# Regrouping the small products of a DeltaNet and maxout kernel between its large ones, with two chunks in one PSUM tile

## The chip, the cores and the metric

The kernel runs on one core of a Trainium2 chip. The time is device microseconds (us) of one execution. The engines are PE (TensorE matrix products; PEld is its weight load), DVE (VectorE), ACT (ScalarE), POOL (GpSimd) and SP (SyncE, which here only issues transfers). Each engine works through its own instructions strictly in order and waits on semaphores for the others. Lower is better.

## The reference

Two stages follow each other. First a delta rule attention, token by token, for 4 batches (B), 8 heads (H), 768 tokens (S) and head size 48 (D):

```python
k_n = k / (norm(k) + 1e-6)
for t in range(S):
    y[:, :, t] = einsum('bhd,bhde->bhe', q[:, :, t], state)
    v_old = einsum('bhde,bhd->bhe', state, k_n[:, :, t])
    state += beta[t] * einsum('bhd,bhe->bhde', k_n[:, :, t], v[:, :, t] - v_old)
```

Then y, seen as 3072 tokens of 384 numbers, goes through a maxout layer of width 768 and an output product:

```python
h = maximum(maximum(x @ w1, x @ w2), x @ w3)
out = h @ w_out
```

All numbers are float32.

## The kernel before

**Attention in chunks.** The 768 tokens are cut into 12 chunks of 64. Inside a chunk, the recurrence becomes the inverse of a triangular matrix per head, so that a chunk needs only small products. A *unit* is one chunk and one half of the batches; 4 units (2 chunks) form a *group*, and there are 6 groups. The names of the steps, which are also the letters in the schedule below, are:

- `t` (`turn_blocks`, L375): transposes of keys and queries on DVE, from the tile `turned` that `load_blocks` (L348, letters `L` and `N`) fetched, into `kqt`.
- `g` (`gram`, L395): products of keys with keys and with queries, PSUM tile `p_g`; DVE makes `pt` from it (L390), ACT `at` (L423), and SP writes `at` to device memory as `at_d` (four transfers a unit, L436).
- `blocks(m)` (L478): one transfer from SP reads `at_d` back as `x_bl` in another layout (L483).
- `solve(m)` (L498): the triangular inverses of the 32-wide blocks. It begins with a norm (ACT's `root_bl`, L261, then a row of short DVE instructions) and goes on in 31 steps of two DVE instructions (L552, L556). Then SP writes `y_d` (L577) and reads it back as `ut` (L586, four transfers a chunk).
- `z` (`join_z`, L694): for each chunk 32 products of 32 x 32 into PSUM tile `p_z` (64 records in the trace, since each product shows as two), then two ACT copies into `z`.
- `d` (`turn_t1`, L615): transposes of `ut` on DVE.
- `j` (`join_u`, L707): 32 products from `z` and `d`'s result into `p_j`, then two ACT multiplications by -1 into `ut`.
- `k`, `q` (`old_k` L738, `old_q` L747): products of keys and queries with the running state, `p_k` and `p_q`; DVE subtracts the one from `v_t` (L743), ACT copies the other (L751).
- `u` (`new`, L753), `s` (`step`, L771), `y` (`to_y`, L793): new values, state update, outputs. `x`, `w`, `X`: y goes through device memory into the layout of the maxout stage, `xt`.

**The maxout stage.** `ffn(m)` (L1150) is a generator over the 512 tokens of group m. Each of its *steps* (a yield) computes one product of 128 x 512 outputs, `p_h`, three products deep (L1161), and its elementwise part: ACT's relu (L1171) on even steps, DVE's maximum (L1175) on odd ones. From group 1 on there are 12 such steps, 0 to 11, and then steps 12 to 19 for the output product `p_o` (L1199). Its PSUM tiles have two buffers, so the product of step 11 needs the maximum of step 9 to be done.

**The order is written by hand.** The outer loop (L1427) runs over m and, behind each step i of `ffn(m)`, calls `links(m + 1, LINKS[i])`: a string of letters with numbers. Letters of the recurrence act on group m + 1, loads and key products on the group after that. While the maxout of one group runs, the recurrence of the next one and the preparation of the one after next are so threaded between its products. Each string that holds products is one *place* of small products between large ones. Besides, the loop issues `blocks(m + 2)` behind step 6, starts `solve(m + 2)` behind step 8, takes three of its steps behind each later step and the last three behind step 0 of the next group.

Groups 1 to 4 run as four similar periods. Group 0 has its own schedule (`EARLY_LINKS`), in which `z` of chunks 2 and 3 stands behind step 18. The last group has no recurrence left.

**PSUM.** The small products share one rotation of three tiles: `ps_two(name)` (L83) gives a tile of 128 x 2 x 512 numbers. A chunk's z or j uses a quarter of a tile on each side: columns 0 to 255 of each of the two parts. A new tile waits until the one three before it has been read.

Of the kernel before, what the change touches and what calls it, by code (L numbers as in the profile page):

```python
# [18 lines left out]
BL = 32  # L19
# [4 lines left out]
def kernel(  # L24
# [31 lines left out]
    nc = tc.nc  # L56

    B, H, S, D = q.shape
# [24 lines left out]
    def ps_two(name):  # L83
        return psum.tile([128, 2, 512], FP32, name=name, tag="two", bufs=3)
# [103 lines left out]
    t1 = [const.tile([128, 2, H, BL], FP32, name=f"t1{i}") for i in range(NU)]  # L188
# [206 lines left out]
    def gram(n, parts=(0, 1), queues=one_queue, copy=nc.scalar.copy, later=False):  # L395
        kqt, g = kqts[n], n % 2
        p_g = ps_two("p_g")

        whole = len(parts) == 2 and not g
        for j in range(NP):  # L400
            for par in range(2):
                for bb in range(2):
                    kq = kqt[dims(par), j, bb ^ g]
                    for i in (0,) if whole else parts:
                        c0 = j * 128 + i * C
                        nc.tensor.matmul(  # L406
                            p_g[
                                rows(bb ^ (g * i)), par, c0 : c0 + C * (1 + whole)
                            ],
                            kq[:, 0],  # L410
                            kq if whole else kq[:, i],
                        )
        p_v = p_g.rearrange("p two (j i t) -> p two j i t", j=NP, i=2)
        if 1 in parts:
            pt = pts[n] = square("pt")
            if later:
                copy(by_par(pt), p_v[:, :, :, 1])
            else:
                masked(pt, p_v[:, :, :, 1])
        if 0 not in parts:  # L420
            return
        at = ats[n] = square("at")
        copy(by_par(at), p_v[:, :, :, 0])  # L423
        if queues:
            to_dram(n, queues)
# [52 lines left out]
    def blocks(m, queue=nc.sync):  # L478
        if m == 1:
            xs[m] = in_wo(0)  # L480
        else:
            xs[m] = work.tile([128, 2, HB * BL + HB], FP32, name="x_bl", bufs=1)
        queue.dma_start(  # L483
            out=in_rows(xs[m]),
            in_=at_d[m].rearrange("c f b h j i -> (c f b h) j i"),
        )
# [125 lines left out]
    def block(bb, f=0, n=BL):  # L612
        return slice(C * bb + BL * f, C * bb + BL * f + n)
# [23 lines left out]
    def heads_of(c, name, w):  # L637


        copies = (nc.scalar.copy,) if c else (nc.scalar.copy, nc.vector.tensor_copy)  # L640
        n = H // len(copies)
        for i, copy in enumerate(copies):
            p_v = ps_two(name)[:, :, 0 : n * w]
            yield (
                range(i * n, i * n + n),
                p_v.rearrange("p g (h x) -> p g h x", x=w), copy,
            )

    def negated_of(c, name, w):
        if c:  # L650
            p_v = ps_two(name)[:, :, 0 : H * w].rearrange("p g (h x) -> p g h x", x=w)
            yield range(H), (p_v, p_v), (nc.scalar.mul,) * 2
            return
        p = [
            ps_two(name)[:, :, 0 : NP * w].rearrange("p g (h x) -> p g h x", x=w)
            for _ in range(3)
        ]
        yield range(NP), (p[0], p[0]), (nc.scalar.mul,) * 2
        yield range(NP, H), (p[1], p[2]), (nc.scalar.mul, nc.vector.tensor_scalar_mul)

    def span(hs):
        return slice(hs[0], hs[-1] + 1)
# [15 lines left out]
    def halves_u(c):  # L678
        t, z = fine.pop(c), zs[c % NU]
        for hs, p_v, negate in negated_of(c, "p_f", BL):  # L680
# [4 lines left out]
            for f in (0, 1):  # L685
                for bb in range(2):
# [4 lines left out]
                        -1.0,  # L691
                    )

    def join_z(c):  # L694
        at = [ats.pop(2 * c + g) for g in range(2)]
        z, second = zs[c % NU], ut[c % NU][:, :, :, BL:C]
        for hs, p_v, _ in heads_of(c, "p_z", BL):
            for i, h in enumerate(hs):
                for bb, g in TILES:
                    r = block(bb, 1)  # L700
                    nc.tensor.matmul(
                        p_v[block(bb ^ g), g, i], at[g][r, h, 0:BL], second[r, g, h]
                    )
            for bb in range(2):
                nc.scalar.copy(z[block(bb), :, span(hs)], p_v[block(bb)])

    def join_u(c):  # L707
        z, t = zs[c % NU], t1[c % NU]
        u12 = ut[c % NU][:, :, :, BL:C]
        for hs, p_v, negate in negated_of(c, "p_j", BL):  # L710
            for i, h in enumerate(hs):
                for bb, g in TILES:
                    r = block(bb ^ g)
                    nc.tensor.matmul(p_v[bb][block(bb), g, i], t[r, g, h], z[r, g, h])  # L714
            for bb in range(2):
                negate[bb](u12[block(bb), :, span(hs)], p_v[bb][block(bb)], -1.0)
# [174 lines left out]
    def both_layers(t):  # L891
        p_m = ps_ffn([128, DM], "p_m")
        for f in range(FT):
            nc.tensor.matmul(  # L894
                p_m,
                w_sb[0][:, t, f * 128 : (f + 1) * 128],
                wo_sb[:, f],
                start=(f == 0),
                stop=(f == FT - 1),
            )  # L900
        nc.scalar.copy(w_sb[0][:, t, 0:DM], p_m)
# [146 lines left out]
    def cross_hidden(i):  # L1048


        n = PAIRS * 128
        w = w_sb[i]
        b11, b12 = w[:, 0, 0:n], w[:, 0, n : 2 * n]
        b21, b22 = w[:, 1, 0:n], w[:, 1, n : 2 * n]
        t = [
            work.tile([128, 2, n], FP32, name="crossed", tag="w_bits", bufs=5)
            for _ in range(2)
        ]
        t1, t2, t3, t4 = (t[n // 2][:, n % 2] for n in range(4))
        for to, a, b in ((t3, b22, b12), (t1, b12, b11), (t2, b22, t1), (t4, b21, t2)):  # L1060
            nc.vector.tensor_tensor(out=to, in0=a, in1=b, op=ALU.subtract)
        thirds[i] = dict(
            b11=b11, b21=b21, b22=b22, t1=t1, t2=t2, t3=t3, t4=t4,
            c1=w[:, 2, 0:n], c2=w[:, 2, n : 2 * n],
        )
# [147 lines left out]
    def some(gen, n):  # L1213
        for _ in range(n):
            if next(gen, gen) is gen:
                break
# [74 lines left out]
    for _ in range(2):  # L1291
        fetch(nc.gpsimd)
    halves_u(0)
    turn_t1(0)
    join_z(0)
    masked(pts[0], by_par(pts[0]))
    placed(1, 2)
    join_u(0)
    masked(pts[1], by_par(pts[1]))
    old_k(0)  # L1300
# [14 lines left out]


    LINKS = {
        0: "k0 q0 t0 L3", 1: "t1", 2: "g0 g1 t2", 3: "z0 z1 d0 d1", 4: "j0 j1 t3 V0",
        5: "g2 g3 p1", 6: "u0 N0", 7: "V1 N1", 8: "s0 y0 N2", 9: "x0", 10: "k1 q1",
        11: "u1 w0", 13: "y1 x1 s1", 14: "X0 w1", 16: "P0", 17: "X1 K0 K1 K2 K3",  # L1320
    }
    LAST_LINKS = {**LINKS, 17: "", 19: "X1"}
# [13 lines left out]

    RECURS = dict(
        z=join_z, j=join_u, k=old_k, q=old_q, u=new, s=step, y=to_y, x=to_x,
        e=halves_z, f=halves_u, d=turn_t1,
    )  # L1340
# [3 lines left out]
        g=lambda n: gram(n, queues=(nc.gpsimd,) * 2 if n in (10, 11) else one_queue),  # L1344
# [3 lines left out]
    def links(m, names):  # L1348
        for name in names.split():
            f, i = name[0], int(name[1])  # L1350
            if f in RECURS and m < GROUPS:
                RECURS[f](2 * m + i)
            elif f in MADE and m + 1 < GROUPS:
                MADE[f](2 * (m + 1) + i)
            elif f in UNIT and m + 1 < GROUPS:
                UNIT[f](4 * (m + 1) + i)
            elif f == "N" and m + 2 < GROUPS:
                load_blocks(4 * (m + 2) + i)
# [68 lines left out]
    for m in range(1, GROUPS):  # L1427
        for i, _ in enumerate(ffn(m)):
            if i == 0:
                some(solving, 3)  # L1430
            if m == 1 and i in (2, 5, 8):
                both_layers(i // 3)
            if m == GROUPS - 2 and i in (4, 5):
                cross_hidden(i - 3)
            if m == GROUPS - 2 and i in (8, 9):
                cross_weights(i - 8)
            if m + 2 < GROUPS:
                if i == 6:
                    blocks(m + 2)
                if i == 8:  # L1440
                    solving = solve(m + 2)
            links(m + 1, (LAST_LINKS if m == GROUPS - 2 else LINKS).get(i, ""))
            if i > 7:
                some(solving, 3 if i > 8 else 1)
# [29 lines left out]
```

## Time and profile before

| | |
|---|---|
| three runs | 513.08, 513.89, 513.96 us; median 513.89 us |
| profiled execution | span 510.5 us from first to last instruction; its own time around it is not given |
| mean granted TensorE clock | 0.966 |
| PE busy | 491.1 us, 96% of the span |
| DVE, ACT, POOL busy | 349.9, 168.7, 192.7 us |
| maxout products `p_h` (L1161) | 187.5 us, x450 |
| output products `p_o` (L1199) | 65.3 and 25.2 us |

How it is read: times are from the start of the span. The chain is followed back from the last instruction, at each step to what released it; its pieces add up to the span. In the timeline, a line gives start, duration, engine, source line, operation, output and inputs, count, and in brackets how long the engine had stood idle before and what ended that. "SPq" is the issue of a transfer by SP, not the transfer. Matrix products are pipelined, and their ends are modelled.

The windows of the four periods: 158.0 to 242.4 us (84.4 us long; it has three further products of the weights, `p_m`, in it), 242.4 to 315.0 (72.6), 315.0 to 387.7 (72.7), and group 4 from 387.7 on, which has no key products.

### The profile page before, as it was taken

The page shows a single profiled execution, that of the slowest core. Times are in us where ns is not written, and L with a number is a line of the kernel's source. Part 1 is how long each engine was busy: PE and PEld are TensorE (multiplying, and loading weights), DVE is VectorE, ACT ScalarE, POOL GpSimd, SP SyncE. Part 2 cuts the span into 40 slices and gives each one's busy share as a digit, 9 for nine tenths or more (in the row PEclk, how much of TensorE's full clock was granted, in tenths as well). Part 3 has the DMA queues.
Part 4 walks back from the last instruction along what each step waited for, and adds up shares of the span by engine and source line. Part 5 has one row for each costly group of instructions (what it writes and reads, how often), then busy time and mean ns, then how long its engine had stood idle before and what let it go on. Part 6 is the DMA issues. An engine that isn't in the chain of part 4 may idle for free.

```text
span 510.5 us, 18528 instructions
## 1 busy us (share of the span) xinstructions
PE 491.1 (96%) x8016; PEld 333.1 (65%) x8016; DVE 349.9 (69%) x801; ACT 168.7 (33%) x320; POOL 192.7 (38%) x317
## 2 busy tenths in 40 slices
PE   7778989999999999999999999999999999999996
PEld 6567778756565565665555565555655556998796
DVE  5897799969996430899563987635897455456752
ACT  5585664884422242210252101252101412113210
POOL 7434372783491926670575770503130000000000
PEclk9755999999999999999999999999999999999999
DMA  8938869764055925353675454923343202230001
GB/s 111 192 64 221 194 151 155 195 199 100 5 148 140 175 46 130 99 143 83 144 136 130 120 137 94 174 37 92 80 116 81 44 3 64 54 71 2 0 17 46
DMA packets 106304, 53.49 MB, mean 105 GB/s; under 512 B 89712, under 2 KB 99984, under 8 KB 106224
## 3 DMA queue, kind: packets, MB, share of 16 engines
q1 hardware_dynamic: 94352, 31.35, 30.4%
q0 software_dynamic: 9472, 20.37, 16.4%
q8 instruction: 63, 1.03, 0.9%
q10 hardware_dynamic: 2400, 0.59, 0.6%
q14 instruction: 17, 0.14, 0.1%
HBM read 39.17 MB, written 13.11 MB: 102 GB/s over the span
## 4 chain that ended last, share of the span: by engine, by line
PE 73%; DVE 14%; DMA 5%; ACT 4%; SPq 2%; issue 2%; POOL 0%; DVEq 0%; ACTq 0%; POOLq 0%
PE p_h L1161 26%; PE p_o L1199 13%; PE p_o L960 9%; PE p_e L1102 3%; DVE tmp L552 3%; PE p_g L406 3%; PE p_c L1102 2%; PE p_m L894 2%; PE p_u L759 2%; DMA kmore<-in_k_dram 2%; PE p_k L731 2%; PE p_y L801 2%; DVE y_bl L556 2%; PE p_s L782 2%; PE p_j L714 1%
## 5 line engine op out<-in xcount | busy, mean ns | idle before, releaser
L1161 PE MATMUL p_h<-xt,w_sb 128*128 128x512 f32 (+1 forms) x450 | 187.5, 558 | 0.7 <-ACT xt L827 0.6
L1161 PEld LDWEIGHTS p_h<-xt,w_sb 128*128 128x128 f32 x450 | 82.3, 193 | 68.7 <-issue 61.8
L1199 PE MATMUL p_o<-wo_sb,h 128*128 128x384 f32 x192 | 65.3, 490 | 0.0
L1175 DVE TENSOR_TENSOR h<-h,p_h 128x512 f32<-128x512 f32 (+1 forms) x42 | 25.4, 606 | 53.9 <-PE p_h L1161 52.8
L552 DVE TENSOR_TENSOR tmp<-x_bl,y_bl 128x31 f32<-128x31 f32 (+20 forms) x139 | 51.3, 369 | 4.1
L556 DVE TENSOR_TENSOR y_bl<-y_bl,tmp 128x31 f32<-128x31 f32 (+20 forms) x139 | 48.5, 349 | 4.8
L1199 PEld LDWEIGHTS p_o<-wo_sb,h 128*128 128x128 f32 x192 | 35.7, 190 | 23.2
L364 POOL DMA_DIRECT2D turned<-in_q_dram x72 | 39.1, 551 | 4.3 <-POOL turned L359 2.9
L1205 ACT COPY o_sb<-p_o 128x384 f32<-128x384 f32 x16 | 7.7, 479 | 85.8 <-PE p_o L1199 79.8
L1171 ACT ACTIVATE h<-p_h 128x512 f32<-128x512 f32 x24 | 14.3, 597 | 63.4 <-PE p_h L1161 60.5
L254 POOL TENSOR_TENSOR w_sb<-mant,up 128x384 int32<-128x384 int32 x18 | 19.1, 1059 | 39.3 <-DVE mant L250 39.2
L406 PEld LDWEIGHTS p_g<-kqt 48*64 48x64 f32 x1216 | 24.6, 142 | 9.0 <-issue 6.4
L406 PE MATMUL p_g<-kqt 48*64 48x64 f32 (+1 forms) x1216 | 27.8, 242 | 0.9 <-ACT kqt L335 0.8
L789 DVE TENSOR_TENSOR st<-st,p_s 48x768 f32<-48x768 f32 (+1 forms) x18 | 17.1, 949 | 15.4 <-PE p_s L782 15.2
L120 POOL DMA_DIRECT2D kpad<-in_k_dram x32 | 21.8, 690 | 14.1 <-issue 12.7
L1199 PE MATMUL p_o<-w_sb,xt 128*128 128x384 f32 x72 | 25.2, 486 | 0.0
L139 POOL DMA_DIRECT2D v_t<-in_v_dram x14 | 11.5, 829 | 35.5 <-PE p_u L759 35.5
L390 DVE TENSOR_TENSOR pt<-p_g,mask 128x512 f32<-128x512 f32 x20 | 13.8, 688 | 15.9 <-PE p_g L406 15.8
L287 POOL TENSOR_TENSOR v_t<-v_t,nrm 128x768 f32<-128x768 f32 x12 | 17.9, 1493 | 9.0 <-DVE nrm L281 8.9
L359 POOL MEMSET turned<- 128x96 f32 x18 | 3.3, 192 | 47.6 <-DVE kqt L380 47.6
L759 PEld LDWEIGHTS p_u<-v_t,ut 64*64 64x64 f32 x768 | 13.4, 141 | 10.1 <-issue 7.8
L1199 PEld LDWEIGHTS p_o<-w_sb,xt 128*128 128x128 f32 x72 | 13.7, 190 | 9.5
(212 smaller groups left out, 837.0 us busy)
## 6 DMA issues: line engine op xcount, KB each, us to landing
out_dram<-o_sb SPq DMA_DIRECT2D x40, 96.0 KB
w_bits<-in_moe_w_dram SPq DMA_DIRECT2D x9, 384.0 KB
w_bits<-in_moe_w_dram POOLq DMA_DIRECT2D x9, 384.0 KB, 5.2
turned<-in_q_dram POOLq DMA_DIRECT2D x72, 48.0 KB, 2.9
kpad<-in_k_dram POOLq DMA_DIRECT2D x32, 96.0 KB, 6.1
y_x<-y SPq DMA_DIRECT2D x16, 192.0 KB
qall<-y_x SPq DMA_DIRECT2D x32, 96.0 KB
v_t<-in_v_dram POOLq DMA_DIRECT2D x14, 192.0 KB, 5.0
```

What stands on the lines that cost most here:

```text
L120: queues[bb].dma_start(out=dst[rows(bb ^ g), :, 0:D], in_=src[2 * bb + g, :, c * C : (c + 1) * C, :].rearrange("h p d -> p h d"),)
L254: nc.gpsimd.tensor_tensor(out=dst.bitcast(I32), in0=mant_v.bitcast(I32), in1=up_v, op=ALU.add)
L364: (queue, nc.gpsimd)[i].dma_start(out=t[p0 : p0 + 32, bb, at : at + NP * 2 * D].rearrange("p (j x) -> p j x", j=NP), in_=(k, q)[i][2 * bb ...
L406: nc.tensor.matmul(p_g[rows(bb ^ (g * i)), par, c0 : c0 + C * (1 + whole)], kq[:, 0], kq if whole else kq[:, i],)
L552: nc.vector.tensor_tensor(out=t_v, in0=row.to_broadcast(t_v.shape), in1=column.to_broadcast(t_v.shape), op=ALU.mult,)
L556: nc.vector.tensor_tensor(out=rest, in0=rest, in1=t_v, op=ALU.subtract)
L759: nc.tensor.matmul(p_v[rows(bb ^ g), g, i], ut[c % NU][rows(bb), g, h], rhs[rows(bb), g, h],)
L960: nc.tensor.matmul(to[:, g], a[j][:, 128 * g : 128 * (g + 1)], b[j], start=(start and g == j == 0), stop=(stop and g == 1 and j == PAIRS - 1),
L1102: nc.tensor.matmul(to, w[stays], moves, start=(n == 0), stop=(n == len(terms) - 1))
L1161: nc.tensor.matmul(p_h, w_sb[i][:, t, f * 128 : (f + 1) * 128], xt[:, t, lo : lo + w], start=(t == 0), stop=(t == KT - 1),)
L1175: nc.vector.tensor_tensor(out=h, in0=h, in1=p_h, op=ALU.max)
L1199: nc.tensor.matmul(p_o, stays, moves, start=(n == 0), stop=(n == len(terms) - 1))
```

## The change

Three edits go together. First, `z` of the two chunks of a group takes one PSUM tile instead of two: the even chunk takes columns 0 to 255 of both parts, the odd one 256 to 511 (from chunk 2 on). The same is done for `j` (from chunk 4 on). Second, the strings of `LINKS` are regrouped: `k0 q0` move from step 0 to step 3, behind `z0 z1 d0 d1`; `g0 g1 t2` from step 2 to step 4, behind `j0 j1`; `t3` from step 4 to step 5; `g2 g3` from step 5 to step 6, behind `u0`. Third, `blocks(m + 2)` moves from step 6 to step 7. The number of places with small products falls from ten (steps 0, 2, 3, 4, 5, 6, 8, 10, 11, 13) to seven (3, 4, 6, 8, 10, 11, 13). The products and elementwise instructions themselves are the same.

```diff
+    shared = {}
+
+    def half_of(c, name):
+        key = name, c // 2
+        p = shared.pop(key) if key in shared else shared.setdefault(key, ps_two(name))
+        at = H * BL * (c % 2)
+        return p[:, :, at : at + H * BL].rearrange("p g (h x) -> p g h x", x=BL)
+
     def join_z(c):
         at = [ats.pop(2 * c + g) for g in range(2)]
         z, second = zs[c % NU], ut[c % NU][:, :, :, BL:C]
-        for hs, p_v, _ in heads_of(c, "p_z", BL):
+        if c < 2:
+            parts = heads_of(c, "p_z", BL)
+        else:
+            parts = [(range(H), half_of(c, "p_z"), None)]
+        for hs, p_v, _ in parts:
...
     def join_u(c):
         z, t = zs[c % NU], t1[c % NU]
         u12 = ut[c % NU][:, :, :, BL:C]
-        for hs, p_v, negate in negated_of(c, "p_j", BL):
+        if c < 4:
+            parts = negated_of(c, "p_j", BL)
+        else:
+            p_j = half_of(c, "p_j")
+            parts = [(range(H), (p_j, p_j), (nc.scalar.mul,) * 2)]
+        for hs, p_v, negate in parts:
...
     LINKS = {
-        0: "k0 q0 t0 L3", 1: "t1", 2: "g0 g1 t2", 3: "z0 z1 d0 d1", 4: "j0 j1 t3 V0",
-        5: "g2 g3 p1", 6: "u0 N0", 7: "V1 N1", 8: "s0 y0 N2", 9: "x0", 10: "k1 q1",
+        0: "t0 L3", 1: "t1", 3: "z0 z1 d0 d1 k0 q0", 4: "j0 j1 g0 g1 t2 V0",
+        5: "t3 p1", 6: "u0 g2 g3 N0", 7: "V1 N1", 8: "s0 y0 N2", 9: "x0", 10: "k1 q1",
         11: "u1 w0", 13: "y1 x1 s1", 14: "X0 w1", 16: "P0", 17: "X1 K0 K1 K2 K3",
     }
...
             if m + 2 < GROUPS:
-                if i == 6:
+                if i == 7:
                     blocks(m + 2)
                 if i == 8:
                     solving = solve(m + 2)
```

## The prediction

> **What bounds the kernel now.** I read the page's busy shares first, then the chain that ended last, then the timeline of single stages.
>
> ```profile
> span 510.5 us, 18528 instructions
> PE 491.1 (96%) x8016; PEld 333.1 (65%) x8016; DVE 349.9 (69%) x801; ACT 168.7 (33%) x320; POOL 192.7 (38%) x317
> ```
>
> TensorE (PE) is busy 96% of the span, so it is the bound, and any wait put into its queue is paid nearly in full. The steady part is four periods, which start at 158.1, 242.5, 315.1 and 387.9 us (I call them periods 1 to 4, after m). Here is the chain of period 3: start, duration, engine, tile, line.
>
> ```profile
> 315.14 2.57 PE p_h L1161 x6
> 317.72 1.08 PE p_k L731 x64
> 318.80 0.93 PE p_q L731 x64
> 319.73 5.35 PE p_h L1161 x12
> 325.08 2.02 PE p_g L406 x94
> 327.10 2.77 PE p_h L1161 x6
> 329.87 1.28 PE p_z L701 x98
> 331.15 2.77 PE p_h L1161 x6
> 333.92 1.39 PE p_j L714 x99
> ```
>
> Two prices stand there. A maxout product lasts 2.57 us behind another and 2.77 us behind small products: 0.19 to leave. The first small group lasts 1.08 us, the next of its kind 0.93: 0.15 to enter. So one place of small products costs 0.34 us beyond its work.
>
> The timeline shows what lies beside PE:
>
> ```profile
> 329.80 1.35 PE L701 MATMUL p_z<-ut,at 32*32 32x32 f32 x128
> 330.60 2.38 ACT L705 COPY z<-p_z 32x512 f32<-32x512 f32 x4 [2.13 <-PE p_z L701]
> ...
> 333.85 1.46 PE L714 MATMUL p_j<-z,t 32*32 32x32 f32 x128
> 333.96 0.60 ACT L1171 ACTIVATE h<-p_h 128x512 f32<-128x512 f32 x1 [0.98 <-PE p_h L1161]
> 334.65 2.40 ACT L716 ACTIVATE ut<-p_j 32x512 f32<-32x512 f32 x4
> ...
> 345.75 0.34 SPq L483 DMA_DIRECT2D x_bl<-at_d  x1
> ...
> 352.45 0.26 ACT L261 ACTIVATE root_bl<-x_bl 128x32 f32<-128x32 f32 x1 [1.58 <-DMA x_bl<-at_d]
> ...
> 358.55 0.30 PEld L1161 LDWEIGHTS p_h<-xt,w_sb 128*128 128x128 f32 x2 [0.22 <-DVE h L1175]
> ```
>
> ScalarE (ACT) starts copying z of the first chunk at 330.60, while PE is still in the second chunk's half of p_z: two tiles, so nobody waits. And x_bl reaches ACT only 6.6 us after its issue; VectorE's work on it ends just in time for PE's product of step 11 at 358.55.
>
> In period 4, z already waits for a transfer, the last load of ut:
>
> ```profile
> 401.64 0.61 PEld L701 LDWEIGHTS p_z<-ut,at 32*32 32x32 f32 x60 [0.25 <-DMA ut<-y_d]
> ```
>
> **The change, part by part.**
>
> *Fewer places.* Periods 1 to 3 lose three places each (steps 0, 2 and 5), period 4 loses one: 10 x 0.34 = 3.4 us. Against that, z and k, and j and g, now follow each other directly in different tile shapes. The nearest row is p_j before p_u in period 0, last weight load of one to first of the next: 0.04 us. With 7 such neighbours I take -3.2, bounds -3.4 and -2.9. [...]
>
> *z and j in one tile.* The built program shows a new wait: the first z product of the odd chunk waits for the second ACT copy of the even chunk's z, and the first j product of the odd chunk for the second ACT negation of the even one's. The halves do not overlap, but they are interleaved in the same two banks, and the framework orders them. Price: the first chunk's 64 records take 0.71 us (half of 1.35 plus its end), ACT starts 0.80 after PE's start (329.80 to 330.60), two of four copies take 1.19, and a release takes 0.08 (a copy of z that ends at 107.48, p_j at 107.56 in period 0). The second half so starts at 0.80 + 1.19 + 0.08 = 2.07 instead of 0.65: 1.42 us each. For j: ACT's relu ends at 334.56, its negations start 0.80 after p_j; two take 1.20: the same. Behind the waiting z stand k, q and all later products. Periods 1 to 3: 6 x 1.42 = +8.5; bounds 1.2 each (copies alone) and 1.5: +7.2 to +9.0.  [...]
>
> *Period 4.* k and q leave step 0 and so no longer cover the wait for ut. z would start 2.2 us earlier (2.01 + 0.19), but ut lands at 401.6 relative to the same VectorE chain: all 2.2 come back as waiting, and z's copy wait hides under it. j adds 1.4. Sum +3.6; bounds +2.6 (ut a microsecond sooner) and +4.1.
>
> *Periods 2 and 3, ut.* z moves forward 4.4 us there (k and q 2.01, g 2.02, two leavings 0.38), and ut of the second chunk, with 3.5 and 4.1 us to spare (issue ends 252.75 and 324.59, landing 1.7 later, second half of z at 257.9 and 330.4), becomes late by 0.9 and 0.3: hidden under the 1.42, so nothing; without that wait they would cost themselves.
>
> *Period 0.* Chunks 2 and 3 share a z tile too (their j do not). There ACT is behind with weight conversion: p_z runs at 103.49, ACT's z copies at 106.29. The second z waits until 107.56 instead of 104.17: 3.4 us on PE. But the chain there runs through ACT and VectorE; followed forward (p_z to 108.3, p_h, p_j 111.1, p_h, p_j and p_u to 116.3, u copy, root_bl), root_bl comes at 117.45 instead of 115.01: I take +2.4, bounds +0.9 (the copies' own delay) and +3.5.
>
> *The x_bl round trip.* g2 and g3 move behind u0 in step 6, x_bl's load to step 7. Before, g ends at 340.11 and step 8 starts at 349.30: 9.2 us. Now p_h, p_h is all that lies between: 5.35. So x_bl comes 3.84 us later against step 8. It first eats VectorE's spare (root_bl's end to nt_bl's start beyond a 0.1 hand-over): at least 2.1 in period 1, 0.6 in 2, 0.3 in 3; then PE's own spare at step 11: 0.5, 0.5, 0. Left: 1.2, 2.7, 3.5. In period 3 the v_t load (issued 344.31) shared the queues with x_bl; it now goes before it, and x_bl may take 4.7 us as in period 2: 1.6. I take 1.2 + 2.7 + 1.6 = +5.5. Bounds: 0, if shorter transfers give the 3.84 back; above, 7.4, and 2 more where the v_t and turned loads (now at the same time as the at_d writes) slow these: in period 1, x_bl was issued 4.4 us after the last write under such loads, in period 3 1.5 us. Behind the waiting ACT stand y_bl's diagonal and the next relu; behind VectorE the maximum that frees the product's bank.
>
> At nothing: t2 and t3 later (VectorE stands idle 3.4 us before its maximum at 338.19, and each has a product of 2.8 us before its g); the queues of SP and POOL, whose issues keep their order (the 16 at_d writes, then x_bl, on SP; v_t and turned loads on POOL), only their times move; the k subtraction between d0, d1 and pt, 0.95 us, ahead of u0 by two products; p_g behind p_k's release in the rotation of three tiles, about 2 us early. Uncovered they would cost their own 1 to 1.4.
>
> Sum: -3.2 + 8.5 + 3.6 + 2.4 + 5.5 = +16.8 us on a span of 510.5, that is 527.3; the three runs' median lies 3.4 above that span (the profiled execution's own time is not given), which I keep: 513.9 + 16.8 = 530.7.
>
> **Rivals.**
> A: x_bl stays hidden, the copy waits alone cost: 530.7 - 5.5 = 525.2. For it: between 340 and 345 the DMA engines are busy at two to five tenths, so the writes could land sooner. Against: period 3 had no spare left at step 11.
> B: the loads collide, VectorE's solve becomes the bound of each period: three times 2 to 3 more, 538. For it: period 1's 4.4; against: period 3 has no turned loads then.
> C, the other side: a place costs more than the chain shows, because matmul ends are modelled. It decides from (16.8 + 3.2) / 10 = 2.0 us a place; at 2.3 the time would be 511. Against it: the pieces of the chain add up to the span, so 0.34 can hardly be 2.
> D: the change does not do what it says, the waits fall on finished copies: -3.2 + 2.2, at 513. Against it: ACT's 1.19 us cannot begin before z ends.
>
> **How the numbers follow.** Forecast (527.5 to 535.5) 0.58, A (522 to 527.5) 0.24, B (535.5 to 541) 0.11, C 0.02, D 0.02, some gain I miss (515 to 522) 0.03. The range 522 to 538 takes forecast, A and the lower half of B: about 0.85. No change is 513.89 within 0.2%, 1.0 us, about what a measurement can tell here. Faster 0.03 (C, half of D), same 0.01 (half of D), slower 0.96.
>
> **What would show it.** Right: in each of periods 1 to 4 p_z and p_j split in two, PE idle about 1.4 us before the second half, released by ACT z and ACT ut; 7 places; p_h of step 11 released by VectorE, later by 1 to 3 us; root_bl waiting on x_bl by 3 us or more. Wrong: p_z of 1.3 us without a gap; root_bl without a wait; or a period 3 of 72.7 us or less.

## The result, and the profile after

The changed kernel takes 558.03 us (median, 553.17 to 562.04) against 513.57 for the kernel before in the same comparison: a ratio of 1.082 between the faster executions, 95% interval 1.077 to 1.087. Slower was right, but the move is +44.5 us (+42 by the ratio) where +16.8 was forecast, and the time lies 20 us above the range. The profiled execution is the slowest one timed (562.04 us, span 560.2, mean TensorE clock 0.921), which the ratio leaves out; the others had nearly the same clock, 0.917 to 0.924, so its profile is read as it stands.

First the page of the changed kernel: span, busy time of PE, the granted TensorE clock in 40 slices (tenths of full speed), and q8, the instruction queue taken for PE's (packets, MB, share; the reason stands under e11 and e12).

```profile
span 560.2 us, 18510 instructions
PE 517.4 (92%) x8016; PEld 348.1 (62%) x8016; DVE 350.3 (63%) x801; ACT 168.3 (30%) x320; POOL 192.7 (34%) x317
PEclk9856999999999689999679999769999879999999
...
q8 instruction: 63, 1.03, 0.8%
```

The same clock line of the kernel before:

```profile
PEclk9755999999999999999999999999999999999999
```

Two things grew. PE idles 42.8 us instead of 19.4 (span less busy time). And PE is busy 26.3 us longer (517.4 against 491.1) with the same 8016 matmuls, and even with fewer places to enter and leave. The clock line says why: before, the clock fell only in the first 53 us (6.8 and 27.3 us at 0.50); now it falls again in every period. The forecast had the first kind of loss alone.

PE's waits of the changed kernel from 95 to 480 us (waited for: us in total, times, longest); before, the same question gives a single line, 1.0 us:

```profile
PE p_z L713 <- ACT z L717: 6.8, 4, 3.0
PE p_j L731 <- ACT ut L733: 5.1, 4, 1.3
PE p_z L713 <- DMA ut<-y_d: 4.4, 2, 2.3
PE p_q L748 <- issue: 2.8, 2, 1.4
PE p_h L1178 <- ACT h L1188: 2.5, 2, 1.3
PE p_u L776 <- issue: 1.0, 2, 0.5
```

The two waits for ScalarE's copies are there as forecast, 1.3 us each (3.0 in period 0). "Issue" is new: PE waits for nothing that the profile shows.

Now the chain of the changed kernel in period 2 (start, duration, engine, tile, line):

```profile
271.74 1.07 PE p_z L713 x60
272.81 1.89 PE p_k L748 x64
274.70 1.71 PE p_q L748 x64
276.40 5.08 PE p_h L1178 x6
281.49 0.70 PE p_j L731 x50
...
283.45 0.75 PE p_j L731 x50
284.20 3.44 PE p_g L406 x96
287.64 7.16 PE p_h L1178 x12
294.80 1.08 PE p_u L776 x64
```

Compare with the chain of period 3 in the prediction: p_k 1.89 for 1.08, p_q 1.71 for 0.93, p_h 5.08 for 2.77, p_g 3.44 for 2.02, two p_h 7.16 for 5.35. None of these waits for anything; they run at a lower clock (0.50 in the windows below), until p_u is back at 1.08.

The granted clock in windows of 3.41 us (window, length, PE busy, PEld, DVE, ACT, POOL, clock, DMA share, GB/s) gives the shape of it:

```profile
267.37:270.78 3.41, 0.78 (x66) 0.56 (x52) 3.18 (x7) 1.15 (x2) 3.17 (x6) 1.00 1.20 192
270.78:274.20 3.42, 2.46 (x116) 2.40 (x119) 0.00 (x0) 1.15 (x2) 1.88 (x5) 0.50 0.49 120
...
277.61:281.02 3.41, 3.41 (x5) 1.08 (x4) 0.00 (x0) 0.00 (x0) 0.44 (x1) 0.50 0.17 43
281.02:284.44 3.42, 2.14 (x141) 1.59 (x144) 0.00 (x0) 1.96 (x4) 0.00 (x0) 1.00 0.00 0
284.44:287.85 3.41, 3.41 (x97) 3.29 (x88) 0.84 (x2) 1.57 (x3) 0.00 (x0) 0.50 0.02 5
287.85:291.26 3.41, 3.41 (x5) 1.34 (x6) 1.87 (x5) 0.59 (x1) 0.00 (x0) 0.50 0.40 64
291.26:294.68 3.42, 3.42 (x9) 1.28 (x7) 2.02 (x5) 0.00 (x0) 0.00 (x0) 1.00 0.11 20
```

In these traces the clock is either 1.00 or 0.50, and it changes only at the edges of such windows. A window in which PE worked 0.78 of 3.41 us is followed by 0.50, and so is one with 2.14 us of work: p_j, the stop of 1.3, p_j and the start of p_g. From 95 us on, the changed kernel spends nine stretches of 3.41, 6.83 or 10.24 us, 61.4 us in all, at 0.50; the kernel before spends none.

### The profile page after: what moved, and what is told of

It is laid out like the page before. It is cut to its first block, busy times and chain, and to the rows that moved or that the text cites. A ratio compares the mean times of both kernels' runs of the same rounds, so it can differ in the third digit from the quotient of the medians.

```text
span 560.2 us, 18510 instructions
## 1 busy us (share of the span) xinstructions
PE 517.4 (92%) x8016; PEld 348.1 (62%) x8016; DVE 350.3 (63%) x801; ACT 168.3 (30%) x320; POOL 192.7 (34%) x317
## 4 chain that ended last, share of the span: by engine, by line
PE 69%; DMA 10%; DVE 9%; ACT 4%; SPq 4%; issue 3%; POOL 0%; DVEq 0%; ACTq 0%; POOLq 0%
PE p_h L1178 25%; PE p_o L1216 12%; PE p_o L977 8%; PE p_g L406 3%; PE p_e L1119 3%; PE p_u L776 2%; PE p_c L1119 2%; PE p_m L911 2%; DVE tmp L552 2%; DMA ut<-y_d 2%; PE p_k L748 2%; DVE y_p L556 2%; PE p_q L748 2%; PE p_y L818 2%; PE p_j L731 2%
## 5 line engine op out<-in xcount | busy, mean ns | idle before, releaser
L1178 PE MATMUL p_h<-xt,w_sb 128*128 128x512 f32 (+1 forms) x450 | 203.1, 600 | 3.1 <-ACT h L1188 2.5
L1178 PEld LDWEIGHTS p_h<-xt,w_sb 128*128 128x128 f32 x450 | 88.7, 206 | 84.6 <-issue 74.6
L556 DVE TENSOR_TENSOR y_bl<-y_bl,tmp 128x31 f32<-128x31 f32 (+20 forms) x139 | 50.5, 363 | 4.8
L406 PE MATMUL p_g<-kqt 48*64 48x64 f32 (+1 forms) x1216 | 32.3, 269 | 0.5 <-ACT kqt L335 0.5
L406 PEld LDWEIGHTS p_g<-kqt 48*64 48x64 f32 x1216 | 29.2, 164 | 5.0 <-issue 2.9
L806 DVE TENSOR_TENSOR st<-st,p_s 48x768 f32<-48x768 f32 (+1 forms) x18 | 17.1, 950 | 14.6 <-PE p_s L799 14.4
L713 PE MATMUL p_z<-ut,at 32*32 32x32 f32 x768 | 11.0, 205 | 11.7 <-ACT z L717 6.8
L717 ACT COPY z<-p_z 32x512 f32<-32x512 f32 (+1 forms) x26 | 14.1, 543 | 20.1 <-PE p_z L713 19.8
```

The source lines that it names most:

```text
L406: nc.tensor.matmul(p_g[rows(bb ^ (g * i)), par, c0 : c0 + C * (1 + whole)], kq[:, 0], kq if whole else kq[:, i],)
L556: nc.vector.tensor_tensor(out=rest, in0=rest, in1=t_v, op=ALU.subtract)
L1178: nc.tensor.matmul(p_h, w_sb[i][:, t, f * 128 : (f + 1) * 128], xt[:, t, lo : lo + w], start=(t == 0), stop=(t == KT - 1),)
```

## The experiments

Three questions: what halves the clock, which part of the change brings it, and what are the "issue" stops? In the table, "stops" are PE's waits of 95 to 480 us less the 1.0 us of the kernel before, "half" is the time at clock 0.50 from 95 us to 480, and "sum" is stops + half/2 - 0.34 for each place saved (3.2 in the four kernels with the whole changed order, as in the prediction) + work added (22.7 us in e3 and 7.6 in e8 for the fillers, 8.0 in e11 and e12). It stands beside what was measured: the profiled execution less the median of the kernel before. That half of the time at 0.50 is lost is an estimate from the chain above, where p_h takes 5.08 us for 2.77.

```
kernel              median  ratio, 95% interval     stops  half   sum  measured
changed             558.03  1.082 (1.077-1.087)     21.6   61.4  49.1   48.5
e1_places_only      541.86  1.056 (1.051-1.062)     14.1   30.7  26.3   27.5
e2_shared_only      536.18  1.046 (1.040-1.051)     12.4   10.2  17.5   17.7
e3_filled           553.65  1.075 (1.066-1.083)      9.8   17.1  37.8   40.1
e4_grams_early      557.75  1.084 (1.078-1.090)     18.1   54.6  43.0   44.3
e5_no_late_ut       531.78  1.039 (1.030-1.047)     11.2   17.1  17.3   17.2
e6_grams_late_only  517.39  1.008 (1.004-1.011)      2.8    3.4   3.5    2.3
e7_kq_move_only     530.89  1.033 (1.025-1.042)      6.7   23.9  17.2   18.9
e8_filled_less      548.72  1.071 (1.064-1.079)     14.7   30.7  34.5   34.0
e9_kq_beside_g      515.34  1.002 (0.998-1.006)      1.5    3.4   1.8    4.7
e10_u_beside_g      514.38  0.999 (0.996-1.002)      2.8    0.0   1.8    6.1
e11_twice_one_run   532.44  1.035 (1.030-1.040)      5.2   10.2  18.3   17.7
e12_twice_two_runs  522.24  1.014 (1.008-1.019)      1.7    6.8  14.5   12.3
```

The sum meets the measurement within 2.3 us in all rows but e9's (2.9) and e10's (4.3). In these two the first z behind 95 us starts at 106.81 and 108.37 us, against 103.49 in the kernel before: most of what is missing was lost ahead of it. So stops and half clock account for the larger differences, and it remains to find where each comes from.

### e1: the order alone

The changed order, but join_z and join_u as before:

```diff
-            parts = [(range(H), half_of(c, "p_z"), None)]
+        for hs, p_v, _ in heads_of(c, "p_z", BL):
...
-            p_j = half_of(c, "p_j")
+        for hs, p_v, negate in negated_of(c, "p_j", BL):
```

> The changed order of the small products (seven places, x_bl's load in step 7), with z and j of the two chunks in separate tiles again. Theory 1 (the granted clock is halved because PE stands still for the copies between the two halves): no such stops here, so the granted clock stays at 1.00 in all four periods; x_bl is issued 23 us after z instead of 16, some of it hidden by the 3.5 to 4.1 us that ut had to spare, so a period of 74 to 76 us and 516 to 525 us in all, 519 taken. Theory 2 (the clock is halved because small products now stand in runs of 3.3 us, z z k q and j j g g, with no full-size product between; the stop is not needed): two stretches at 0.50 in every period as in the changed kernel, about 540 us.

Measured: 541.86 us, +28, as theory 2 has it, but with one half-clock stretch in each period (3.4, 10.2, 10.2 and 6.8 us long) instead of two. There is no stop for copies; what PE does wait for is ut (7.8 us) and "issue" (4.4 us). And a run of small products by itself did no harm here:

```profile
258.57:261.98 3.41, 0.51 (x34) 0.31 (x20) 2.91 (x7) 1.15 (x2) 3.18 (x6) 1.00 1.06 182
261.98:265.40 3.42, 2.65 (x123) 2.59 (x124) 0.00 (x0) 1.15 (x2) 2.27 (x6) 0.50 0.51 125
...
272.22:275.64 3.42, 3.42 (x225) 3.08 (x224) 0.69 (x1) 2.87 (x5) 0.00 (x0) 1.00 0.02 5
```

The last window holds 3.0 us of p_j and p_g without a stop, and the clock stays at 1.00 behind it (the next products last 5.35 for two). The first holds a wait for ut, and the clock halves. Neither theory holds as written: the order alone costs most of the loss, yet not by the length of the runs as such.

### e2: the shared tiles alone

The kernel before with the changed join_z and join_u (half_of) and nothing else.

> The kernel before, ten places and x_bl's load in step 6, with z and j of both chunks in one tile. Theory 1: two stops of 1.4 us in each period and each followed by a stretch at 0.50 of 3.4 us or a multiple: 513.6 + 11.4 for the stops + 3 in period 0 + 14 to 27 for the clock, 541 to 555 us, 545 taken. Theory 2: the runs of small products are short here (1.4 and 2 us), so the clock stays at 1.00 and only the stops are paid: 528 us.

Measured: 536.18 us. PE's waits are as the prediction priced them:

```profile
PE p_z L713 <- ACT z L717: 8.3, 5, 3.3
PE p_j L731 <- ACT ut L733: 5.1, 4, 1.3
```

That is 13.4 us; the prediction's stops were 8 x 1.42 + 3.4 = 14.8. But in the profiled execution only one of the eight stops in periods 1 to 4 is followed by half clock. Two that are not:

```profile
184.54:187.96 3.42, 2.16 (x90) 1.41 (x78) 3.23 (x9) 2.30 (x4) 3.42 (x7) 1.00 0.74 140
187.96:191.37 3.41, 2.25 (x68) 1.02 (x66) 1.04 (x4) 1.71 (x4) 0.75 (x2) 1.00 0.63 100
```

Their busy time, 2.16 and 2.25 us, is that of the 2.14 us window above that halved the clock. The difference is what PE worked on: here 1.28 and 1.56 us of it are full-size products, there 0.47. So theory 1 falls too: a stop of 1.3 us was not enough beside so much full-size work.

Putting every window of 3.413 us between 95 and 480 us of the fourteen profiles side by side (PE's busy time from the windows, the share of full-size products from the timeline): 45 windows at full clock are followed by half clock. In each, PE stood still for 0.59 us or more and full-size products (p_h, p_o, p_m, p_w) had at most 1.35 us. 15 windows with under 0.6 us of full-size products but no stop kept the clock, and so did 10 windows with stops of 0.8 us or more and at least 1.4 us of full-size products. So in these profiles the half clock came only where the two stood in one window, small products and a stop. That was not always enough: 18 windows within the limits of the 45 (still for 0.59 us or more, full-size products at most 1.35 us) kept the clock, among them one of e5 (from 125.20 us) with a stop of 0.97 us and no full-size product, where the small ones are p_k, p_y and p_q. What decides in between is open; the shapes of the small products may count.

### e3 and e8: work in place of the stop

One unused product ahead of the odd chunk's z and j in periods 1 to 4 of the changed kernel:

```diff
+        p_w = ps_ffn([128, TOK], "p_w")
+        for _ in range(3):        # e8: range(1)
+            nc.tensor.matmul(p_w, ident, w_sb[1][:, 0, 0:TOK])
```

> The changed kernel, with three more products of 128x512 (1.3 us, result unused) ahead of the odd chunk's z and of its j in periods 1 to 4, so that PE works while it would wait for the copies; the waits themselves stay. Theory 1: the granted clock stays at 1.00 from 115 us on, apart from waits for ut; the stops cost what they did but nothing more: 534 to 542 us, 537 taken. Theory 2: the runs of small products are the same, the stretches at 0.50 stay, 553 to 560 us.

> The changed kernel with one unused full-size product of a third of p_h's work (0.9 us by p_h's rows) ahead of the odd chunk's z and j in periods 1 to 4, so that the stop shrinks from 1.4 to 0.5 us and nothing is added to its length. Theory C: most stretches at 0.50 go, those that stay follow a wait for ut or an unexplained stop; PE's products take 10 to 20 us less: 536 to 548 us. If the clock were no cause but a consequence of nothing here, the time would stay at that of the changed kernel, 553 to 562 us.

The filler of e3 was mis-sized: three such products last 2.84 us, not 1.3, so it added about 1.5 us to each of the eight stops. Measured: 553.65 and 548.72 us. PE's busy time in e8, and its waits for the copies from 155 to 480 us:

```profile
PE 508.4 (93%) x8032; PEld 340.5 (62%) x8032; DVE 353.3 (65%) x801; ACT 168.2 (31%) x320; POOL 192.5 (35%) x317
...
PE p_j L740 <- ACT ut L742: 0.9, 4, 0.2
PE p_z L721 <- ACT z L725: 0.6, 3, 0.2
```

The time at half clock falls from 61.4 us to 17.1 and 30.7. In e8 PE's waits for the copies in periods 1 to 4 shrink to 1.5 us in sum, its busy time falls from 517.4 to 508.4 though the fillers are in it, and the kernel is 9 us faster. The stretches that stay follow waits for ut (5.2 us) and "issue" (4.2 us). So the half clock does hang on the stops, and costs time: e8 does more work in less time. Its stops are 6.9 us less and its fillers 7.6 us more, which nearly cancel; 30.7 us less at half clock, half of it lost, are 15.4 us, and the profiled executions differ by 14.6. The 548.72 lies just outside the 536 to 548 of theory C, since these other stops remained.

### e4: is it the round over x_bl?

```diff
-        4: "j0 j1 g0 g1 t2 V0", 5: "t3 p1", 6: "u0 g2 g3 N0",
+        4: "j0 j1 g0 g1 t2 t3 V0", 5: "g2 g3 p1", 6: "u0 N0",
...
-                if i == 7:
+                if i == 6:
                     blocks(m + 2)
```

> The changed kernel with t3 in step 4, g2 and g3 back in step 5 and x_bl's load in step 6; everything else as changed, also the shared tiles. Loop theory (a period cannot be shorter than the round z, g, x_bl, VectorE's solve, ut, next z): x_bl's issue comes one product and u0 earlier, 2.8 to 3.6 + 1.1 us, and each of three periods is shorter by as much: 544 to 546 us. Sum theory (PE's own queue sets the period and x_bl costs only PE's wait at step 11, 1.2 us in the changed kernel): three times 1.2 less, about 554 us.

Measured: 557.75 us, no change. In period 2 x_bl is issued 28.1 us after the second half of z instead of 33.6, and ScalarE's waits for x_bl fall from 9.3 us to 3.3; but z still waits 5.0 us for ut, and the half clock is 54.6 us. The loop theory is refuted as a sole bound. Against z, ut did not move at all: from the first of its loads to the start of z it is 5.2 us in period 2 of both kernels (261.92 to 267.15, and 263.63 to 268.86). That fits VectorE's solve, whose steps stand at fixed places between the maxima and so keep step with PE's products; no run tests this by itself.

### e5 and e7: a run of z, k and q

e7 is the kernel before with k0 and q0 behind z1 (step 0 to step 3) and nothing else. e5 has them ahead of z0, g0 and g1 behind j1 in step 4, g2 and g3 in step 5 as before, seven places less in all, and separate tiles:

```diff
-        0: "k0 q0 t0 L3", 1: "t1", 2: "g0 g1 t2", 3: "z0 z1 d0 d1", 4: "j0 j1 t3 V0",
+        0: "t0 L3", 1: "t1", 3: "k0 q0 z0 z1 d0 d1", 4: "j0 j1 g0 g1 t2 t3 V0",   # e5
+        0: "t0 L3", 1: "t1", 2: "g0 g1 t2", 3: "z0 z1 d0 d1 k0 q0", 4: "j0 j1 t3 V0",   # e7
```

> Seven places and separate tiles, but k and q ahead of z in step 3 (2 us more for ut to land), t3 in step 4, g2 and g3 in step 5, x_bl's load in step 6: the same runs of small products of over 3 us, without a late ut. Theory C (the granted clock is halved after a stretch of 3.4 us in which PE both stood still for 0.8 us or more and had under 1.2 us of full-size products; neither suffices alone): no stop, so no half clock in periods 1 to 4, and the time is 513.9 less the places' 3.2, 510 to 515 us. Theory R (a run of small products of over 3 us suffices): at least one stretch at 0.50 in each period, 525 us or more.

> The kernel before with k0 and q0 moved from step 0 behind z1 in step 3, nothing else. By the prediction's terms: four places less (-1.4), ut in time in periods 1 to 3, 2.2 us late in period 4: 514.7 us. Theory C: half clock only where z waits for ut, so at most once in period 4 (1.7 us more): 513 to 517 us. Theory R: the run z z k q of 3.3 us brings a stretch at 0.50 in every period: 522 us or more.

Measured: 531.78 and 530.89 us. Moving two products of 1 us costs 17 us. PE's waits in e5:

```profile
PE p_z L701 <- issue: 6.3, 3, 2.8
PE p_z L701 <- DMA ut<-y_d: 1.5, 1, 1.5
```

and in e7:

```profile
PE p_z L701 <- DMA ut<-y_d: 3.5, 4, 1.1
PE p_k L731 <- issue: 1.5, 1, 1.5
PE p_q L731 <- issue: 1.4, 2, 1.1
```

The "issue" stops lie in the middle of a tile's 64 matmuls, wherever in the run of z, k and q these stand: in p_q and p_k when z goes first, in p_z when k and q do. Late data would stop the same tile in both orders, so it fits badly; the run's length fits. In e7, ut is late as well, in periods 2 to 4. Theory C had not foreseen them; theory R gave the right size, though not the reason.

### e11 and e12: the length of a run, with no data in play

In the kernel before, k0's and q0's matmuls are issued twice into the same tiles in the periods; in e12 q0 moves one step on, so that a full-size product parts the two:

```diff
-        for j in range(NP):
+        for j in range(NP * twice):
+            j %= NP
...
-        0: "k0 q0 t0 L3", 1: "t1", 2: "g0 g1 t2",
+        0: "k0 t0 L3", 1: "t1 q0", 2: "g0 g1 t2",      # e12 only
```

> The kernel before with the matmuls of k0 and q0 in step 0 of the periods issued twice into the same tiles (same result): one run of some 256 small matmuls with no data to wait for, 2.0 us of work more in each of four periods. Supply theory: 513.9 + 8.0 and a stop of 1.1 to 2.9 us with a stretch at 0.50 of 3.4 us (1.7 us lost) in each period: 530 to 540 us. Data theory: 522 us at clock 1.00.

> The same doubled k0 and q0, but q0 moved to step 1, so that a full-size product stands between the two and no run has more than some 130 matmuls; one place more in each period (0.34). Supply theory: 513.9 + 8.0 + 1.4 = 523 us at clock 1.00, without stops. Data theory: the same, 523 us.

Measured: 532.44 against 522.24 us, for the same work and one place more in the faster one. The timeline of e11:

```profile
248.59 2.08 PE L732 MATMUL p_k<-st,kqt 48*64 48x48 f32 x128
250.49 0.52 PE L732 MATMUL p_q<-st,kqt 48*64 48x48 f32 x23
252.28 1.96 PE L732 MATMUL p_q<-st,kqt 48*64 48x48 f32 x105 [1.27 <-issue]
254.17 4.25 PE L1162 MATMUL p_h<-xt,w_sb 128*128 128x512 f32 x6
```

and of e12:

```profile
252.62 2.08 PE L732 MATMUL p_k<-st,kqt 48*64 48x48 f32 x128
254.63 2.84 PE L1162 MATMUL p_h<-xt,w_sb 128*128 128x512 f32 x6
257.41 2.08 PE L732 MATMUL p_q<-st,kqt 48*64 48x48 f32 x128
259.42 2.84 PE L1162 MATMUL p_h<-xt,w_sb 128*128 128x512 f32 x6
```

In e11 PE stops after 128 + 23 matmuls, and the product behind it runs at half clock (4.25 for 2.84). This happens in three of the four periods: stops of 1.27, 2.39 and 1.31 us, each followed by 3.41 us at 0.50. e12 has neither in its four periods. 5.0 us of stops and 10.2 / 2 of half clock, less four places (1.4), are 8.7 of the 10.2 us between them.

The instruction queue points to what PE waits for. The number of its 16 KB packets goes with the number of PE's instructions: the 63 of the page above for 2 x 8016 are 254 to a packet, and the 67 of e11 and e12 for 2 x 8528 are 255. So q8 is taken for PE's queue; that is an estimate from these counts. In these nine "issue" stops, PE went on 2.3 to 3.1 us after a packet of this queue appeared (packets located to 0.25 us):

```
kernel  packet at  PE goes on at      kernel   packet at  PE goes on at
e11     249.50     252.28             e7       340.25     343.00
e11     329.00     331.65             e5       178.00     180.33
e11     407.25     410.04             e5       339.00     342.06
e7      261.00     263.94             e9       327.75     330.55
changed 180.50     183.18
```

In all fourteen profiles there are 35 "issue" stops from 95 to 480 us. 30 of them end 2.3 to 2.9 us after the start of a packet, though packets come only every 8 us on average. 28 of the 30 fall behind 109 to 242 matmuls of a run of 160 to 256; two, of 0.4 and 0.7 us, fall in period 0 at the end of a run of 32. The other five, 0.5 us each, stand ahead of the first matmul of p_u and are of another kind.

A small matmul of k or q with its weight load takes 15 to 16 ns (the 128 of p_k in e12: 2.01 us to the next product), so by this estimate a packet's 255 instructions last about 2 us, less than the 2.7 us from packet to restart. In e12 packets come at such moments too (254.75, 330.25), but there the full-size product of 2.84 us, 12 instructions, runs and PE does not stop. That PE waits for what these packets bring is the author's estimate from this timing and these counts; no trace shows it.

Most packets come without a stop: of the 63 of the changed kernel, two lie behind such a stop from 95 to 480 us. The longest of the 30 stops lasts 2.9 us.

### e6, e9 and e10: single moves

```diff
-        5: "g2 g3 p1", 6: "u0 N0",
+        5: "p1", 6: "u0 g2 g3 N0",          # e6, with blocks(m + 2) at 7
+        5: "g2 g3 u0 p1", 6: "N0",          # e10
...
-        0: "k0 q0 t0 L3", 1: "t1", 2: "g0 g1 t2",
+        0: "t0 L3", 1: "t1", 2: "k0 q0 g0 g1 t2",     # e9
```

> The kernel before with g2 and g3 behind u0 in step 6 and x_bl's load in step 7, nothing else. By the prediction's term x_bl costs 5.5 us (bounds 0 and 9.4): 519 us, at clock 1.00. Loop theory (the round from z over x_bl to the next ut sets the period): x_bl comes 3.8 us later each time, ut's 3.5 to 4.1 us of spare take it up, 514 to 517 us. Theory C: no half clock unless z waits for ut; theory R: the run u0 g2 g3 of 3.1 us brings one stretch at 0.50 in each of three periods, 520 us or more.

> The kernel before with k0 and q0 moved from step 0 to step 2, ahead of g0 g1: one place less per period, and a run of small products of about 220 matmuls, but no late ut and no shared tile. Supply theory (PE stops for its own instructions in a run of more than some 165 to 240 small matmuls, 1.1 to 2.9 us, 2.3 to 3.1 us after a packet of the instruction queue starts; such a stop inside such a run then halves the clock): stops and a stretch at 0.50 in two or more of the four periods, 519 to 530 us. Data theory (the stops inside the runs are late data that the profile does not name, from the later z and ut): nothing is late here, so four places less, 512.5 us at clock 1.00.

> The kernel before with u0 moved from step 6 to step 5, behind g2 g3: one place less in three periods, run of about 160 matmuls, x_bl's load as before. Supply theory: short enough, no stop in most periods; 3 x 0.34 less, 512.8 us, at worst one stop and one stretch at 0.50, 516. Data theory: u0 one product sooner could wait for the negations that fill ut (2.4 us behind j, one product of 2.8 between), so nothing; 512.8 us.

e6 measures the x_bl move with three places less: +3.9 us (interval 2.1 to 5.6), against 5.5 - 1.0 by the prediction's terms. PE's wait is one that the prediction named, a late relu behind ScalarE's wait for x_bl: 2.6 us, one of them 2.4, followed by 3.4 us at half clock, which cost 1.7 more.

e9 was to show stops in two or more periods and 519 us at least. It shows one stop (1.3 us in p_g) and one half-clock stretch, and 515.34 us: no difference from the kernel before that could be measured. So a run of 220 stopped less often than the 256 of e7, e5 and e11; with g's run the supply theory was too pessimistic. e10 shows one such stop as well, 1.3 us in p_u behind 147 of a run of 160, and no half clock.

e9 and e10 were also attempts at a faster kernel, with four and three places less. Neither is: 1.002 (0.998 to 1.006) and 0.999 (0.996 to 1.002). No kernel here beats the one before.

## Why the prediction was wrong

**What was right.** The new waits, their place and their length: 1.42 us each were forecast, 1.3 measured, 13.4 us in e2 against 14.8. The x_bl term is right in kind: ScalarE waits for x_bl over 4 us in periods 2 and 3 (9.3 in all), but PE only 2.5 us (5.5 forecast), for ScalarE's relu and not for VectorE's maximum. The forecast's waits add up to 20.0 us (16.8 + 3.2), and the changed kernel's stops to 21.6. That the sums are so near is partly luck: the copies are 11.9, ut 4.4, "issue" 3.8 (forecast at nothing) and the relu 2.5, less the 1.0 of before.

**The term that was missing.** All terms were priced at the clock of the profile before, 1.00 from 53 us on, as if it were a constant. The stops together with the small products beside them halve it: 61.4 us at half clock, about 27 us of PE's time (30.7, or 26.3 + some of the places' saving). This is the step of the prediction that failed: a constant clock, with nothing in the sum for a slower one. It is about all of the 28 us between +16.8 and +44.5.

**"Fewer places", -3.2 us.** This term priced only entering and leaving; what gathering does besides is far larger and has the other sign. In e1 the order alone costs 28 us, where the prediction's terms for it (places, x_bl, ut in period 4) would give -3.2 + 5.5 + 2.2 = 4.5. A gain from the 0.34 a place never appeared by itself (e9, e10). What the term left out stands between e11 and e12: with a full-size product between the two runs of 128, the 5.0 us of stops and the 10.2 us at 0.50 did not come in the periods.

**"Periods 2 and 3, ut: nothing".** z waited for ut in both, 4.4 us in sum, without cover. The 4.4 us by which z starts earlier were right: ut's first load is issued 9.6 us ahead of z in period 2 before, and 5.2 us in the changed kernel. What was wrong is the landing "1.7 later". That fits period 4 (399.96 to 401.59), where the DMA engines are busy 0.55 of the time. In periods 2 and 3 they are busy throughout (0.99 and 1.01 behind ut's issue in the kernel before), and in the changed kernel ut lands 5.7 and 3.7 us after its issue ends:

```profile
247.61 5.14 SPq L586 DMA_DIRECT2D ut<-y_d  x8
257.20 1.35 PE L701 MATMUL p_z<-ut,at 32*32 32x32 f32 x128
...
261.92 4.04 SPq L586 DMA_DIRECT2D ut<-y_d  x8
267.15 0.75 PE L713 MATMUL p_z<-ut,at 32*32 32x32 f32 x64
271.74 1.07 PE L713 MATMUL p_z<-ut,at 32*32 32x32 f32 x60 [2.33 <-DMA ut<-y_d]
```

(The first two lines are of the kernel before.) So the spare was less than the 3.5 and 4.1 us taken. e7 shows it by itself: there z starts only 2.2 us earlier, and waits for ut in both periods.

**Period 0 and period 4.** The second z of period 0 waited 3.0 us, 3.4 forecast. In period 4 the 2.2 us for ut did not come; z's copy wait (1.3), an "issue" stop (1.4) and two stretches of half clock stood there instead.

**The trace's own time.** A span stands 1.8 to 1.9 us below the time of the same execution in all profiles here, not 3.4. The median was kept as the base, so only the way there was off.

**The rivals.** A, C and D all lay below the result. B reached 538 by a busier VectorE; the time went past it by another way. A clock that falls was no rival at all, although the profile before shows it at 0.50 in its first 53 us, for 34.1 us in which PE stands still for 5.0 us and p_h has 5.1 of the 29.1 us of work. Nor does it take a window that is mostly idle: one in which PE was busy 2.83 of 3.41 us, all but 0.81 of them with small products, was also followed by half clock (e7).

## What to carry to other kernels

Where PE is the bound, look at the granted clock of the whole span before pricing a stop: here a stop of 1 to 2 us among small matmuls was in many windows followed by 3.4 us or more at 0.50, 1.7 us or more on top by the estimate at the table, and one full-size product ahead of each of eight stops took the time at 0.50 from 61.4 us to 30.7 (e8). Long runs of tiny matmuls were not free to gather here: spread between full-size products, runs of up to 128 were not stopped midway in the four periods, while runs of 160 to 256 sometimes were, and 256 in one run cost 10 us more than twice 128. When a reordering looks free by counting work, move one group alone and look at PE's waits for "issue".

## What the runs showed that was not expected

- The clock in the fourteen profiles has two values, 1.00 and 0.50, and changes on a grid of 3.413 us (18 windows of the changed kernel are 61.44 us) whose first edge behind 100 us lies anywhere from 100.04 us (e11) to 103.07 (e9); the stretches from 95 us on last one, two or three windows. That the same kernel differs by several us from one execution to the next (changed kernel 553 to 562, e2 531.7 to 537.4, e3 546.1 to 554.1) would follow from where the grid falls on the stops; this is argued, only one execution of each was profiled. In e2 and e3 the fastest execution has the highest mean clock (0.954 against 0.946 to 0.949, and 0.972 against 0.951 to 0.954). But the kernel before, at full clock from 53 us on in its profile, spreads as far in 23 later executions (511.1 to 518.5), so that is not all.
- PE's busy time alone does not tell which windows keep the clock: 2.16 us busy with 1.28 of full-size work kept it (e2, from 184.54 us), 2.63 us busy with none lost it (changed kernel, from 178.63 us). One window of e5 (from 125.20 us), 2.44 us busy with small products alone, kept it.
- PE stops for up to 2.9 us inside runs of 160 to 256 matmuls of 10 to 21 ns (period 3 of the kernel before: p_z 128 in 1.28 us, p_g 96 in 2.02), and goes on 2.3 to 2.9 us after the start of a packet of q8, the queue taken for its instructions.
